# Attention output made transposed by column tiles of TensorE, the token scale moved to the last copy, no identity product, a new program order

## Chip, cores, metric

One core of one Trainium2 chip. The metric is device time in microseconds (us) of one execution; lower is better. Engines: PE is TensorE's matmul stream, PEld its weight loads, DVE the vector engine, ACT the scalar engine, POOL the general-purpose engine, SPq the queue that issues most DMA transfers.

## The reference, cut to what matters

```python
# attention: q, k, v, alpha of (4, 8, 768, 48); state is 48 x 48 for each batch and head
for t in range(S):
    state = alpha[:, :, t, :, None] * state + np.einsum('bhd,bhe->bhde', k[:, :, t], v[:, :, t])
    y[:, :, t] = np.einsum('bhd,bhde->bhe', q[:, :, t], state)
# x = y as 3072 tokens by 384 features
h = np.maximum(np.maximum(x @ w1, x @ w2), x @ w3)     # 384 -> 768
return h @ w_out                                        # 768 -> 384
```

## The kernel before

The sequence is cut into six chunks of 128 tokens and the batch into two pairs, which gives twelve steps; each step has two halves (u = 0, 1), one batch element with eight heads each. A step goes through PE in pieces: decay sums (`lps`), turning q and k (`tps`), scores (`aps`), attention output (`yps`), turning it back (`xtp`), state update (`sps`), the three gate products (`gps`, 54 matmuls of 256 columns) and the output product (`ops`). Program order on each engine is written out by hand in strings, one letter for each piece.

```python
    def attend(s, u):
        ...
        yps = ps.tile([P, HP, 2, D], FP32, name="yps", tag="s", bufs=2)
        for p in range(HP):                                  # four pairs of heads
            if cb > 0:
                nc.tensor.matmul(yps[:, p], qkT[:, 0, p, :], st[:, p, :], start=True, stop=False)
            for i in range(2):
                nc.tensor.matmul(yps[:, p, i, :], lat[:, i, p, :],
                                 vt[:, u * H + 2 * p + i, :],
                                 start=(cb == 0), stop=(cb == 0 or i == 1))
        xb = work.tile([P, DM], FP16, name="xb", tag="xb")
        nc.scalar.mul(xb, yps.rearrange("p a b d -> p (a b d)"), ys_c)   # token scale: one number per partition
        y_of[s, u] = xb

    def turn_back(s, u):
        ...
        for f in range(NF):
            nc.tensor.transpose(xtp[:, u, f, :], xb[:, f * P:(f + 1) * P], ident)
        if u == 1:
            ...
            nc.scalar.copy(out=xT.rearrange("p f u t -> p u f t"), in_=xtp_of.pop(s))

    def update(s, u):
        ...
        if cb > 0:                                           # the identity product: adds the old state
            nc.tensor.matmul(sps.rearrange("p a b d -> p (a b d)"), ident,
                             st.rearrange("p a b -> p (a b)"), start=True, stop=False)
        for p in range(HP):
            nc.tensor.matmul(sps[:, p], qk[:, 1, u * HP + p].rearrange("p a b -> p (a b)"),
                             vt[:, u * H + 2 * p:u * H + 2 * p + 2, :], ...)
        nc.vector.tensor_mul(stn..., sps, gm...)
    # ... cut ...
    STEADY = """N0 T0 S0 T1 G0 G1 D0 S1 O1 A0 O0 G2 A1 G3 Y0 G4 D1 G5 Y1 G6 X0 X1 G7 M0 V0 G8"""
    # ... cut ...
    load(1)          # load(0) stands further up; each loads alpha, k, q, v of one step
    load(2)
    load_weights()   # nine gate weights, three output weights
    load(3)
    load(4)
```

Of the kernel before, what the change touches and what calls it, by code (L numbers as in the profile page):

```python
# [9 lines left out]
FP32 = mybir.dt.float32  # L10
# [9 lines left out]
SIGMA = float(np.log(256.0))  # L20
# [3 lines left out]
def kernel(  # L24
# [17 lines left out]
    P = 128  # L42
    NCB = S // P
# [7 lines left out]
    assert DM == H * D and NT == B * S and 2 * D <= P  # L51
# [9 lines left out]
    c16_np = np.concatenate([tri_np, ident_np, mask_np, w2_np], 1)  # L61
    at = LAM * (rr - MID)
    c32_np = np.stack(
        [at, -at, np.exp(at + SIGMA), np.exp(-at - SIGMA), rr < 64, rr >= 64], 1
# [3 lines left out]
    raw = ctx.enter_context(tc.tile_pool(name="raw", bufs=4))  # L68
# [5 lines left out]
    ins = {n: t.rearrange("b h s d -> s b h d")  # L74
           for n, t in (("a", alpha), ("q", q), ("k", k), ("v", v))}
    raws = {}
# [4 lines left out]
    def load(s):  # L81
        cb, b0 = where(s)
        for n in ("a", "k", "q", "v"):
            t = raw.tile([P, NH, D], FP32, name=f"r{n}", tag=f"r{n}")
            nc.sync.dma_start(  # L85
                t, ins[n][cb * P:(cb + 1) * P, b0:b0 + U].rearrange("s b h d -> s (b h) d"))
            raws[s, n] = t

    c16 = cpool.tile([P, 3 * P + 2], FP16, name="c16")
    c32 = cpool.tile([P, 6], FP32, name="c32")  # L90
    load(0)
    nc.scalar.dma_start(c16, nc.inline_tensor(c16_np, name="c16").ap())
    nc.scalar.dma_start(c32, nc.inline_tensor(c32_np, name="c32").ap())
    tri, ident, mask, w2 = c16[:, :P], c16[:, P:2 * P], c16[:, 2 * P:3 * P], c16[:, 3 * P:]
    at_c, nat_c, vs_c, ys_c = (c32[:, i:i + 1] for i in range(4))
    half_c = c32[:, 4:6]


    NQ = 4
    las = [cpool.tile([P, NP, 2, 64], FP16, name=f"la{i}") for i in range(NQ)]  # L100
    qks = [cpool.tile([P, 2, NP, 2, 64], FP16, name=f"qk{i}") for i in range(NQ)]

    def clear_padding(i):
        nc.vector.memset(las[i].rearrange("p a b c -> p (a b) c")[:, :, D:], 0.0)
        nc.vector.memset(qks[i].rearrange("p i a b c -> p (i a b) c")[:, :, D:], 0.0)
# [3 lines left out]


    wcat = cpool.tile([P, NF, 3, DF], FP16, name="wcat")
    wo16 = cpool.tile([P, NJ, DM], FP16, name="wo16")
    wstage = []

    def load_weights():
        for jg in range(NJ // 2):
            for g, w in enumerate((moe_w1, moe_w2, moe_w3)):
                cs = slice(jg * 2 * P, (jg + 1) * 2 * P)
                t = cpool.tile([P, NF, 2 * P], FP32, name=f"ws{jg}_{g}")
                nc.sync.dma_start(t, w.rearrange("(f p) j -> p f j", p=P)[:, :, cs])  # L120
                wstage.append((wcat[:, :, g, cs], t))
        for i in range(3):
            js = slice(2 * i, 2 * i + 2)
            t = cpool.tile([P, 2, DM], FP32, name=f"wos{i}")
            nc.sync.dma_start(t, moe_w_out.rearrange("(j p) m -> p j m", p=P)[:, js])
            wstage.append((wo16[:, js], t))

    def cast_weights(_, i):
        for dst, src in wstage[3 * i:3 * i + 3]:
            nc.gpsimd.tensor_copy(out=dst, in_=src)  # L130

    qk_of, v_of, gate_of, qkT_of, lat_of, y_of, xtp_of, xT_of, hT_of, h_of = (
        {} for _ in range(10))

    def logs(s, _):
        la = las[s % NQ].rearrange("p a b c -> p (a b) c")
        nc.scalar.activation(out=la[:, :, :D], in_=raws.pop((s, "a")), func=AFT.Ln)

    def decays(s, u):

        la, qk = las[s % NQ], qks[s % NQ]
        laf = la.rearrange("p a b c -> p (a b) c")
        qk_of[s] = qk
        hs = slice(u * H, (u + 1) * H)
        lps = ps.tile([P, 512], FP32, name="lps", tag="w", bufs=2)
        nc.tensor.matmul(lps[:, :H * D], tri, laf[:, hs, :D], start=True, stop=True)  # L146
        if u == 1:
            for p in range(NP):
                nc.tensor.matmul(lps[:, H * D + 2 * p:H * D + 2 * p + 2],  # L149
                                 la[:, p].rearrange("p a b -> p (a b)"), w2,  # L150
                                 start=True, stop=True)
        ac = work.tile([P, H, D], FP32, name="ac", tag="ac")
        ic = work.tile([P, H, D], FP32, name="ic", tag="ic")
        lv = lps[:, :H * D].rearrange("p (h d) -> p h d", d=D)
        nc.scalar.activation(out=ic, in_=lv, func=AFT.Exp, bias=nat_c, scale=-1.0)  # L155
        nc.scalar.activation(out=ac, in_=lv, func=AFT.Exp, bias=at_c)  # L156
        qv, kv = (qk[:, i].rearrange("p a b c -> p (a b) c")[:, hs, :D] for i in range(2))
        eng = nc.vector if s < 3 else nc.gpsimd
        eng.tensor_mul(kv, raws[s, "k"][:, hs], ic)  # L159
        eng.tensor_mul(qv, raws[s, "q"][:, hs], ac)  # L160
        if u == 1:
            ge = work.tile([P, NP, 2], FP32, name="ge", tag="ge", bufs=6)
            nc.scalar.activation(
                out=ge, in_=lps[:, H * D:H * D + 2 * NP].rearrange("p (a b) -> p a b", b=2),
                func=AFT.Exp)
            gate_of[s] = ge

    def values(s, _):
        vt = work.tile([P, NH, D], FP16, name="vt", tag="vt", bufs=4)
        nc.scalar.mul(vt, raws.pop((s, "v")), vs_c)  # L170
        v_of[s] = vt

    def turn(s, u):

        qk = qk_of[s]
        tps = ps.tile([P, 2, HP, P], FP16, name="tps", tag="w", bufs=2)
        for i in range(2):
            for p in range(HP):
                nc.tensor.transpose(  # L179
                    tps[:, i, p, :],  # L180
                    qk[:, i, u * HP + p].rearrange("p a b -> p (a b)"), ident)
        qkT = work.tile([P, 2, HP, P], FP16, name="qkT", tag="qkT", bufs=3)
        nc.vector.tensor_copy(out=qkT, in_=tps)  # L183
        qkT_of[s, u] = qkT

    def scores(s, u):
        qkT = qkT_of[s, u]
        lat = work.tile([P, 2, HP, P], FP16, name="lat", tag="lat")
        aps = [ps.tile([P, HP, P], FP32, name=f"aps{i}", tag="w", bufs=2) for i in range(2)]
        for p in range(HP):  # L190
            for i in range(2):
                rows = slice(64 * i, 64 * i + D)
                nc.tensor.matmul(aps[i][:, p, :], qkT[rows, 1, p, :], qkT[rows, 0, p, :],  # L193
                                 start=True, stop=True)
        for i in range(2):
            nc.vector.tensor_mul(lat[:, i], aps[i],  # L196
                                 mask.unsqueeze(1).broadcast_to([P, HP, P]))
        lat_of[s, u] = lat

    def attend(s, u):  # L200
        cb, b0 = where(s)
        st, vt = sts[b0 + u][cb % 2], v_of[s]
        qkT, lat = qkT_of.pop((s, u)), lat_of.pop((s, u))
        yps = ps.tile([P, HP, 2, D], FP32, name="yps", tag="s", bufs=2)
        for p in range(HP):
            if cb > 0:
                nc.tensor.matmul(yps[:, p], qkT[:, 0, p, :], st[:, p, :],  # L207
                                 start=True, stop=False)
            for i in range(2):
                nc.tensor.matmul(yps[:, p, i, :], lat[:, i, p, :],  # L210
                                 vt[:, u * H + 2 * p + i, :],
                                 start=(cb == 0), stop=(cb == 0 or i == 1))
        xb = work.tile([P, DM], FP16, name="xb", tag="xb")
        nc.scalar.mul(xb, yps.rearrange("p a b d -> p (a b d)"), ys_c)  # L214
        y_of[s, u] = xb

    def turn_back(s, u):
        if u == 0:
            xtp_of[s] = ps.tile([P, U, NF, P], FP16, name="xtp", tag="s", bufs=2)
        xtp, xb = xtp_of[s], y_of.pop((s, u))  # L220
        for f in range(NF):
            nc.tensor.transpose(xtp[:, u, f, :], xb[:, f * P:(f + 1) * P], ident)  # L222
        if u == 1:
            xT = work.tile([P, NF, U, P], FP16, name="xT", tag="xT", bufs=3)
            nc.scalar.copy(out=xT.rearrange("p f u t -> p u f t"), in_=xtp_of.pop(s))  # L225
            xT_of[s] = xT

    gm_of = {}

    def gates(s, _):  # L230

# [7 lines left out]
    def update(s, u):  # L239

        cb, b0 = where(s)
        qk, vt = qk_of[s], v_of[s]
        gm = gm_of[s]
        st, stn = sts[b0 + u][cb % 2], sts[b0 + u][(cb + 1) % 2]
# [138 lines left out]
```

## Time and profile before

| | before |
|---|---|
| median, range of three runs | 170.75 us (170.47 to 171.71) |
| profiled span | 168.8 us |
| PE busy | 156.9 us, 93% |
| steady step | 11.93 us |
| first gate matmul | 30.51 us |

The page of the profile before. The digits are busy tenths in 40 slices of the span; PEclk is the granted TensorE clock in tenths.

```profile
PE 156.9 (93%) x1758; PEld 121.1 (72%) x1758; DVE 112.2 (66%) x185; ACT 99.0 (59%) x181; POOL 49.0 (29%) x72
...
PE   7955859999999999999999999999999999999992
...
PEclk9995675599999999999999999999999999999999
```

PE is full from the seventh slice to the last but one. Before that there are holes, and the granted clock is lower.

The table of busy time by stretch, before. Columns: stretch, its length, busy time of each engine with its count of instructions, granted clock, DMA share, GB/s.

```profile
core 0: us, PE busy (x) PEld busy (x) DVE busy (x) ACT busy (x) POOL busy (x), PEclk, DMA share, GB/s
...
10.00:20.00 10.00, 6.46 (x71) 4.23 (x72) 7.03 (x13) 4.80 (x9) 0.00 (x0) 0.67 1.38 218
20.00:30.60 10.60, 7.93 (x94) 5.60 (x92) 7.89 (x14) 7.17 (x13) 3.25 (x6) 0.66 1.01 274
...
87.40:99.35 11.95, 11.95 (x150) 9.64 (x148) 8.78 (x15) 8.13 (x16) 4.28 (x6) 1.00 1.03 207
```

In the steady stretch only PE is full, so there a microsecond saved on PE's stream is a microsecond saved, and a microsecond saved on another engine is worth nothing.

PE's timeline before, some of the groups that the change touches. Columns: start, duration from first start to last end, engine, line, operation, count. The durations overlap, because matmuls are pipelined: the cost of a group is the distance from its start to the start of the next.

```profile
89.64 0.82 PE L268 MATMUL gps_1589<-xT,wcat 128*128 128x256 f16 x6
90.39 0.23 PE L193 MATMUL aps_1598<-qkT 48*128 48x128 f16 x1
...
90.72 0.83 PE L268 MATMUL gps_1610<-xT,wcat 128*128 128x256 f16 x6
91.39 0.21 PE L207 MATMUL yps<-st_1_89,qkT 128*128 128x96 f16 x1
...
91.77 0.82 PE L268 MATMUL gps_1634<-xT,wcat 128*128 128x256 f16 x6
...
94.46 0.55 PE L222 MATMUL xtp<-c_68,xb 128*128 128x128 f16 x6
94.85 0.82 PE L268 MATMUL gps_1702<-xT,wcat 128*128 128x256 f16 x6
...
96.61 0.33 PE L247 MATMUL sps<-st_0_92,c_68 128*128 128x384 f16 x1
96.77 0.33 PE L250 MATMUL sps<-vt,qk_85 128*128 128x96 f16 x4
```

Six gate matmuls take 0.655 us (54 take 5.90). So the scores of one half cost 90.72 - (89.64 + 0.655) = 0.42 us, the gap before them included, and its attention output 91.77 - (90.72 + 0.655) = 0.395 us. Turning back costs 94.85 - 94.46 = 0.39 us per step, an identity product 96.77 - 96.61 = 0.16 us.

The queue's timeline before: the first weight is the thirteenth transfer.

```profile
21.73 1.52 SPq L120 DMA_DIRECT2D ws_0_114<-in_moe_w_dram  x1
```

### The profile page before, as it was taken

How to read it: one execution, taken by the hardware profiler on the slowest of the kernel's cores; microseconds unless marked ns; L12 is line 12 of the kernel's file. 1: busy time of each engine (PE TensorE's matmuls, PEld its weight loads, DVE VectorE, ACT ScalarE, POOL GpSimd, SP SyncE). 2: the span in 40 equal slices, each digit the busy share in tenths (PEclk: the TensorE clock that was granted, in tenths of full speed). 3: DMA queues.
4: the chain of work that ended last, by engine and by line, in shares of the span. 5: the costliest groups of instructions: out<-in, count | busy, mean ns of one | idle time of the engine just before them, and what ended most of it. 6: DMA issues, size and time to landing. Idle time of an engine off the chain costs nothing.

```text
span 168.8 us, 4329 instructions
## 1 busy us (share of the span) xinstructions
PE 156.9 (93%) x1758; PEld 121.1 (72%) x1758; DVE 112.2 (66%) x185; ACT 99.0 (59%) x181; POOL 49.0 (29%) x72
## 2 busy tenths in 40 slices
PE   7955859999999999999999999999999999999992
PEld 2423637699887676886877978968968869869860
DVE  4186777756647757597587587687667775975730
ACT  3616585142777684874974964956856748435232
POOL 0000005756063454404512531541442244100000
PEclk9995675599999999999999999999999999999999
DMA  6999999998999999999897967948931011020013
GB/s 131 223 219 218 176 247 336 355 360 170 226 172 213 218 248 254 192 226 221 219 223 189 235 105 177 228 91 192 212 92 50 0 56 41 0 93 4 0 47 140
DMA packets 107251, 28.68 MB, mean 170 GB/s; under 512 B 99808, under 2 KB 107232, under 8 KB 107232
## 3 DMA queue, kind: packets, MB, share of 16 engines
q1 hardware_dynamic: 106944, 28.32, 77.3%
q8 instruction: 13, 0.21, 0.6%
q10 hardware_dynamic: 288, 0.10, 0.3%
q14 instruction: 6, 0.05, 0.1%
HBM read 23.69 MB, written 4.72 MB: 168 GB/s over the span
## 4 chain that ended last, share of the span: by engine, by line
PE 81%; SPq 7%; DMA 3%; ACT 3%; DVE 2%; issue 1%; ACTq 0%
PE ops L285 14%; SPq L85 7%; PE tps L179 6%; DMA ra<-in_alpha_dram 3%; PE yps L210 3%; PE xtp L222 2%; PE lps L146 2%; PE yps L207 2%; PE sps L250 2%; PE sps L247 2%; DVE lat L196 1%; PE lps L149 1%; ACT xb L214 1%; PE gps_514 L268 1%; PE gps_523 L268 1%
## 5 line engine op out<-in xcount | busy, mean ns | idle before, releaser
L268 PEld LDWEIGHTS <-wcat 128*128 128x128 f16 x648 | 60.3, 98 | 9.0 <-POOL gm L235 0.2
L285 PE MATMUL ops<-wo_97,hT 128*128 128x384 f16 x144 | 27.1, 327 | 0.0
L288 ACT COPY ob<-ops 128x384 f32<-128x384 f32 x24 | 11.5, 480 | 14.2 <-PE ops L285 14.2
L155 ACT ACTIVATE ic<-lps,c_69 128x384 f32<-128x384 f32 x24 | 13.9, 581 | 8.4 <-PE lps L146 5.1
L285 PEld LDWEIGHTS <-hT 128*128 128x128 f16 x144 | 12.8, 98 | 7.5
L183 DVE COPY qkT<-tps 128x1024 f16<-128x1024 f16 x24 | 16.4, 683 | 1.3 <-PE tps L179 1.1
L214 ACT ACTIVATE xb<-yps,c_69 128x384 f16<-128x384 f32 x24 | 14.0, 585 | 4.8 <-PE yps L210 4.8
L156 ACT ACTIVATE ac<-lps,c_69 128x384 f32<-128x384 f32 x24 | 13.8, 575 | 0.0
L210 PE MATMUL yps<-vt,lat 128*128 128x48 f16 x192 | 12.2, 190 | 0.6 <-ACT vt L170 0.6
L193 PEld LDWEIGHTS <-qkT 48*128 48x128 f16 x192 | 6.3, 98 | 8.8 <-issue 7.7
L159 POOL TENSOR_TENSOR qk_87<-rk,ic 128x384 f16<-128x384 f32 x6 | 6.0, 997 | 21.9 <-ACT ic L155 21.9
L210 PEld LDWEIGHTS <-lat 128*128 128x128 f16 x192 | 10.5, 101 | 1.5 <-DVE lat L196 0.7
L170 ACT ACTIVATE vt<-rv,c_69 128x768 f16<-128x768 f32 x12 | 11.3, 940 | 0.0
L225 ACT COPY xT<-xtp 128x768 f16<-128x768 f16 x12 | 9.6, 803 | 1.0 <-PE xtp L222 1.0
L296 PE MATMUL wps<-blank 128*128 128x512 f16 x22 | 8.0, 528 | 1.2 <-DVE blank L343 1.2
L159 POOL TENSOR_TENSOR qk_86<-rk,ic 128x384 f16<-128x384 f32 x4 | 4.0, 997 | 15.4 <-ACT ic L155 15.4
L130 POOL CAST wcat<-ws_0_114 128x768 f16<-128x768 f32 x1 | 0.8, 823 | 26.3 <-DMA ws_0_114<-in_moe_w_dram 26.3
L159 POOL TENSOR_TENSOR qk_85<-rk,ic 128x384 f16<-128x384 f32 x4 | 4.0, 995 | 13.9 <-ACT ic L155 13.9
L207 PEld LDWEIGHTS <-qkT 128*128 128x128 f16 x80 | 7.7, 98 | 0.4
L222 PE MATMUL xtp<-c_68,xb 128*128 128x128 f16 x72 | 7.4, 228 | 0.5 <-ACT xb L214 0.3
L159 POOL TENSOR_TENSOR qk_84<-rk,ic 128x384 f16<-128x384 f32 x4 | 4.0, 996 | 12.4 <-ACT ic L155 12.4
L222 PEld LDWEIGHTS <-xb 128*128 128x128 f16 x72 | 5.2, 101 | 2.3 <-ACT xb L214 0.9
(409 smaller groups left out, 359.6 us busy)
## 6 DMA issues: line engine op xcount, KB each, us to landing
ra<-in_alpha_dram SPq DMA_DIRECT2D x12, 384.0 KB, 4.7
rk<-in_k_dram SPq DMA_DIRECT2D x12, 384.0 KB, 5.6
rq<-in_q_dram SPq DMA_DIRECT2D x12, 384.0 KB, 5.8
rv<-in_v_dram SPq DMA_DIRECT2D x12, 384.0 KB, 5.7
out_dram<-ob SPq DMA_DIRECT2D x24, 192.0 KB, 2.0
ws_0_114<-in_moe_w_dram SPq DMA_DIRECT2D x1, 384.0 KB, 4.9
ws_1_116<-in_moe_w_dram SPq DMA_DIRECT2D x1, 384.0 KB, 4.5
ws_2_118<-in_moe_w_dram SPq DMA_DIRECT2D x1, 384.0 KB, 5.0
```

The lines of the kernel that those rows point to most:

```text
L85: nc.sync.dma_start(t, ins[n][cb * P:(cb + 1) * P, b0:b0 + U].rearrange("s b h d -> s (b h) d"))
L155: nc.scalar.activation(out=ic, in_=lv, func=AFT.Exp, bias=nat_c, scale=-1.0)
L156: nc.scalar.activation(out=ac, in_=lv, func=AFT.Exp, bias=at_c)
L159: eng.tensor_mul(kv, raws[s, "k"][:, hs], ic)
L170: nc.scalar.mul(vt, raws.pop((s, "v")), vs_c)
L183: nc.vector.tensor_copy(out=qkT, in_=tps)
L210: nc.tensor.matmul(yps[:, p, i, :], lat[:, i, p, :], vt[:, u * H + 2 * p + i, :], start=(cb == 0), stop=(cb == 0 or i == 1))
L214: nc.scalar.mul(xb, yps.rearrange("p a b d -> p (a b d)"), ys_c)
L222: nc.tensor.transpose(xtp[:, u, f, :], xb[:, f * P:(f + 1) * P], ident)
L268: nc.tensor.matmul(gps[:, j, :], wcat[:, f, g, jj * P:(jj + 1) * P], xT[:, f].rearrange("p u t -> p (u t)"), start=(f == 0), stop=(f == NF ...
L285: nc.tensor.matmul(ops, hT_of[s][:, jj, u * P:(u + 1) * P], wo16[:, jj, :], start=(jj == 0), stop=(jj == NJ - 1))
L288: nc.scalar.copy(out=ob, in_=ops)
```

## The change

The intent: (1) make the attention output with features on the partitions at once, so that it need not be turned back. Features come in blocks of 32 (a pair of heads has 96), and each block is a product with 32 stationary columns that goes to one of four column tiles of PE. (2) With tokens now along the free axis, a scale per token is no longer one number per partition; it moves to the last copy, where tokens are on partitions again. The maxima in between are not affected by a positive factor. (3) The old state is added on DVE, not by an identity product. (4) Load order and program order are new: weights come in between the inputs, more warm-up matmuls stand in the prologue, and the two halves' scores, and the two halves' attention outputs, stand next to each other.

```diff
-SIGMA = float(np.log(256.0))
+SIGMA = float(np.log(16.0))
+    LOADS = """a1 a0 q0 w0 k0 k1 q1 w2 v0 a2 v1 w1
+        w3 w4 w6 w5 q2 k2 w7 w8 v2 a3 w11 w10
+        w9 q3 k3 v3"""
     # ... cut: the exponents' biases go into the scale of the logarithm ...
-        nc.scalar.mul(xb, yps.rearrange("p a b d -> p (a b d)"), ys_c)
-            nc.tensor.transpose(xtp[:, u, f, :], xb[:, f * P:(f + 1) * P], ident)
+        yps = bank([P, NF, P], "yps", tag or "s")
         for f in range(NF):
+            jobs = []
+            for c in range(P // C):
+                p, part = divmod(P // C * f + c, 3)
+                vp = vt[:, u * HP + p].rearrange("p a b -> p (a b)")
+                job = [] if cb == 0 else [(st[:, p, C * part:C * (part + 1)], qkT[:, 0, p, :])]
+                # ... cut: one or two products of v with lat ...
+                jobs.append(job)
+            for n in range(max(len(j) for j in jobs)):
+                for c, job in enumerate(jobs):
+                    if n < len(job):
+                        nc.tensor.matmul(yps[C * c:C * (c + 1), f, :], job[n][0], job[n][1],
+                                         start=(n == 0), stop=(n == len(job) - 1))
     # update
-            nc.tensor.matmul(sps.rearrange("p a b d -> p (a b d)"), ident,
-                             st.rearrange("p a b -> p (a b)"), start=True, stop=False)
+            nc.vector.tensor_add(full, sps_of.pop((s, u)), sts[b0 + u][cb % 2]...)
     # store
-        nc.scalar.copy(out=ob, in_=ops)
+        times(eng or "a", ob, ops_of.pop((s, u)), ys_c)
-    STEADY = """N0 T0 S0 T1 G0 G1 D0 S1 O1 A0 O0 G2 A1 G3 Y0 G4 D1 G5 Y1 G6 X0 X1 G7 M0 V0 G8"""
+    STEADY = """S1@-1 S0g@-1 N0@2 T1@1 t1@1 s0@-1 s1@-1 O0@-1 T0@1 G0@0 t0@1 G3@0
+        z0v@-1 A1@1 a2@1 A0g@1 z1p@-1 O1@-1 o0v@-1 h0@0 a0@1 c0@2 h3@0 G1@0
+        ... Y0@1 h1@0 h2@0 h4@0 f1@2 q0p@2 k0p@2 V0@2 Y1@1 G5@0 ..."""
     # ... cut: prologue, last step, pieces split into matmul and copy, v padded to 64 per head ...
```

In the strings a capital letter is a PE piece (G, O, T, A, Y, S) or an ACT one (N logarithm, V values); small letters are the copies that follow. `Y0` and `Y1` have only work of other engines between them, so on PE they are neighbours; likewise `A1` and `A0`.

## The prediction

> **What bounds the kernel now.** TensorE. The page has PE busy 93% of a 168.8 us span; the busy table by stretch shows PE busy 11.95 of 11.95 us in a steady step (87.4 to 99.35 us), against DVE 8.8, ACT 8.1, POOL 4.3. From start-to-start distances in PE's timeline a steady step is: 54 gate matmuls 5.90, output product 1.95, turning q and k 0.90, scores 2 x 0.42, attention output 2 x 0.395, decay sums 0.53, turning back 0.39, state update 2 x 0.33 (half of it the identity product): 11.96, the step found. So in the steady part only PE stream time counts. The rest is the start: gates begin at 30.6 us, because the first weight lands at 26.7 us behind twelve input loads, 1.75 us apart on the DMA queue; from 10 to 30 us the granted clock is 0.67. Of the 165.5 us to the last matmul about 141 are that stream, about 25 idle, warm-up or slow clock. The tail (3.3 us) stays.
>
> **What the change does.**
> - Removes turning back (0.39 us per step) and the identity product (2 x 0.163): -0.72. Both halves' scores now stand together: one pair of row-tile switches less, about -0.1 (a score group takes 0.42 us, its eight matmuls 0.25).
> - Attention output becomes 28 matmuls per half, 32 columns by 128, instead of 12. With four column tiles side by side, about nine rounds of 56 ns: 0.5 us per half. If the pairs of weight load and matmul follow one another at the 25 ns that the two-column sums show: 0.7. Both halves are back to back, so one switch in and out, about 0.2. Sum 1.2 to 1.7 against 0.79: +0.4 to +0.9. The Trainium skill, TensorEngine Tiling (Array Packing), Key Properties and Restrictions, says that changing the tiling mode drains the engine and that column tiling excludes Fast Weight Load; no trace here shows column tiles yet, the row-tiled scores agree with about 0.1 us per switch.
> - Steady step: 11.5 to 12.0 us, centre 11.7 (-2.5 us over ten steps).
> - The state sum goes to DVE (0.55 each), half the decays to POOL. DVE rises to 9.5 to 10.5 us of the step, ACT falls to about 7 (copies of 2 x 0.48 for 2 x 0.585 and 0.80). Neither should bound.
> - Loads: the first weights are 4th, 8th and 12th, landing near 10, 16 and 23 us by the same spacing (input 1.75, weight 1.13). Gates can start near 21 us and be dense from 24, with two steps' attention done before. Non-useful PE time falls from 25 to between 17 and 20: -5 to -8 us. 57 warm-up matmuls instead of 22 fill idle time and hold the clock.
>
> **Critical path.** The start and the steady PE difference lie on it wholly; the moved scale, copies and exponent biases do not.
>
> **Predicted time:** 162.0 us, 157.0 to 168.0 for 8 times in 10. Faster by over 2%: 0.87; within 2%: 0.10; slower: 0.03.
>
> **What would show each step.** First gate matmul at 20 to 22 us, dense by 25. Clock above 0.67 from 10 to 30 us. Steady step 11.5 to 12.0 us, PE still full, attention 1.2 to 1.7 us for both halves. Last matmul to end about 3.3 us.
>
> **What would make it wrong.** Column-tile weight loads that do not overlap (60 ns per pair would be 3.4 us per step: slower than before). DVE, near 10 of 11.7 us, becoming the one waited for, so that PE has gaps. Weights landing later than the spacing says, or the early order stalling on one late load. A better case: tiles fully side by side and no drain, a step near 11.2.

## The result, and the profile after

| | before | after |
|---|---|---|
| median (lowest to highest) of four runs each | 171.23 us (170.47 to 172.37) | 160.01 us (159.89 to 160.21) |
| profiled span | 168.8 us | 158.9 us |
| PE busy | 156.9 us, 93% | 150.5 us, 95% |
| steady step | 11.93 us | 11.27 us |
| first gate matmul | 30.51 us | 21.97 us |

The ratio is 0.9338, 95% interval 0.929 to 0.9387.

The page after:

```profile
PE 150.5 (95%) x2057; PEld 114.9 (72%) x2057; DVE 126.5 (80%) x210; ACT 78.5 (49%) x153; POOL 62.6 (39%) x87
...
PE   7999998979699999999999999999999999999991
...
PEclk9999999999999999999999999999999999999999
```

More matmuls and less PE time; DVE and POOL took work, ACT lost some. The early 9s of PE are mostly warm-up matmuls.

Busy time by stretch, after, with columns as above:

```profile
10.00:21.97 11.97, 11.39 (x148) 6.53 (x146) 9.00 (x14) 6.36 (x12) 6.00 (x6) 1.00 1.14 214
21.97:34.00 12.03, 10.60 (x136) 8.82 (x133) 9.00 (x16) 7.31 (x14) 5.90 (x8) 1.00 0.96 263
34.00:46.00 12.00, 10.43 (x159) 8.39 (x157) 8.50 (x14) 7.28 (x14) 4.24 (x6) 1.00 1.03 253
...
87.12:98.39 11.27, 11.27 (x174) 9.17 (x174) 10.49 (x18) 5.78 (x14) 5.09 (x8) 1.00 1.11 221
```

The steady step is still full on PE, with DVE at 10.49 of 11.27 us. Between 22 and 46 us PE lacks 1.4 and 1.6 us.

PE's timeline after, around one pair of scores and one of attention outputs:

```profile
91.90 1.47 PE L322 MATMUL gps<-xT,wcat 128*128 128x256 f16 x12
93.30 0.62 PE L235 MATMUL aps<-qkT 48*128 48x128 f16 x16
93.85 1.15 PE L346 MATMUL ops<-wo,hT 128*128 128x384 f16 x6
...
96.02 1.47 PE L322 MATMUL gps<-xT,wcat 128*128 128x256 f16 x12
97.42 0.24 PE L271 MATMUL yps<-qkT,st 128*32 128x128 f16 x4
97.49 0.23 PE L271 MATMUL yps<-lat,vt 128*32 128x128 f16 x4
...
97.83 0.23 PE L271 MATMUL yps<-qkT,st 128*32 128x128 f16 x4
...
98.32 1.92 PE L322 MATMUL gps<-xT,wcat 128*128 128x256 f16 x16
```

Twelve gate matmuls take 12 x 0.109 = 1.31 us. So the scores of both halves cost 93.85 - (91.90 + 1.31) = 0.64 us, where two separate groups cost 0.84; and attention of both halves costs 98.32 - (96.02 + 1.31) = 0.99 us, where it was 0.79 before plus 0.39 for turning back. The four tiles start together and each round takes about 0.06 us; the second half starts at 97.83, 0.41 us after the first, which is seven rounds.

The queue after; the first weight is the fourth transfer:

```profile
4.39 2.14 SPq L99 DMA_DIRECT2D ws<-in_moe_w_dram  x1
```

Where the ten microseconds went, from PE's timelines:

| part | before | after | difference |
|---|---|---|---|
| start, until the first piece of step 3 | 60.25 | 55.35 | -4.9 |
| eight steady steps, 3 to 10 | 95.24 | 90.13 | -5.1 |
| last step, until PE's last output product ends | 9.97 | 9.99 | 0.0 |

(Steps are counted from 0. Step 3 begins with its first turning or state product; the last step begins with its first gate matmul, at 155.49 us before and 145.48 us after; PE ends at 165.46 and 155.47 us.) The rest after PE's end is 3.3 and 3.4 us.

### The profile page after: what moved, and what is told of

The parts are those of the page before. It is cut to its first block, busy times and chain, and to the rows that moved or that the text cites. A ratio compares the mean times of both kernels' runs of the same rounds, so it can differ in the third digit from the quotient of the medians.

```text
span 158.9 us, 4886 instructions
## 1 busy us (share of the span) xinstructions
PE 150.5 (95%) x2057; PEld 114.9 (72%) x2057; DVE 126.5 (80%) x210; ACT 78.5 (49%) x153; POOL 62.6 (39%) x87
## 4 chain that ended last, share of the span: by engine, by line
PE 64%; SPq 20%; DMA 10%; ACT 3%; issue 1%
PE gps L322 36%; SPq L87 13%; PE ops L346 13%; DMA ra<-in_alpha_dram 10%; SPq L99 7%; PE yps L271 5%; PE tps L221 4%; PE aps L235 2%; PE sps L292 2%; PE lps L175 1%; ACT la L168 1%; PE lps L178 1%; ACT qkT L138 1%; ACT vt L144 1%; ACT xT L138 0%
## 5 line engine op out<-in xcount | busy, mean ns | idle before, releaser
L322 PE MATMUL gps<-xT,wcat 128*128 128x256 f16 x648 | 77.7, 273 | 0.7 <-POOL wcat L140 0.5
L248 DVE TENSOR_TENSOR lat<-aps,c 128x512 f16<-128x512 f32 x48 | 30.5, 681 | 1.1 <-PE aps L235 1.0
L138 ACT CAST h<-gps 128x512 f16<-128x512 f32 x25 | 14.5, 585 | 34.0 <-PE gps L322 33.5
L337 DVE TENSOR_TENSOR h<-gps,h 128x512 f16<-128x512 f32 x36 | 24.5, 684 | 7.0 <-ACT h L138 3.4
L203 POOL TENSOR_TENSOR qk<-rk,ic 128x384 f16<-128x384 f32 x19 | 19.7, 1036 | 25.7 <-ACT ge L196 20.8
L337 DVE TENSOR_TENSOR hT<-gps,h 128x512 f16<-128x512 f32 x36 | 24.7, 690 | 5.5 <-PE gps L322 3.4
L346 PE MATMUL ops<-wo,hT 128*128 128x384 f16 x144 | 26.9, 327 | 0.0
L203 POOL TENSOR_TENSOR qk<-rq,ac 128x384 f16<-128x384 f32 x21 | 21.7, 1037 | 11.2 <-ACT ge L196 7.0
L221 PE MATMUL tps<-c,qk 128*128 128x128 f16 x192 | 14.7, 219 | 1.2 <-DVE qk L203 0.9
L221 PEld LDWEIGHTS <-qk 128*128 128x128 f16 x192 | 11.9, 97 | 3.8 <-DVE qk L203 1.3
```

The source lines that it names most:

```text
L138: nc.scalar.copy(out=dst, in_=src)
L203: engines[eng or "p"].tensor_mul(dst.rearrange("p a b c -> p (a b) c")[:, :, :D], src[:, u * H:(u + 1) * H], dec)
L221: nc.tensor.transpose(tps[:, i, p, :], qk[:, u * NP + i * HP + p].rearrange("p a b -> p (a b)"), ident)
L248: nc.vector.tensor_mul(lat, aps_of[s, u][i], m)
L322: nc.tensor.matmul(gps[:, j, :], wcat[:, f, g, jj * P:(jj + 1) * P], xT[:, f].rearrange("p u t -> p (u t)"), start=(f == 0), stop=(f == NF ...
L337: nc.vector.tensor_max(h, gps, h_of[s, i - 1])
```

## The experiments

All are edits of the kernel after, but for one. Times are medians; ratios are against the kernel before on the same chip. The runs e1, e2, e3 and e8 on one chip and e4, e5, e6, e10 on a second had no unaltered kernel after beside them; after_again stood beside e7, e11 and e12 on a third. So a difference of some tenths of a us between times of different calls is not to be read; the steady steps can be compared.

| run | median us | ratio | interval | steady step us |
|---|---|---|---|---|
| e1_identity | 162.23 | 0.9542 | 0.9488 to 0.9596 | 11.59 |
| e2_old_attention | 162.78 | 0.9567 | 0.9516 to 0.9618 | 11.34 |
| e3_apart | 163.17 | 0.9598 | 0.9551 to 0.9645 | 11.70 |
| e8_tile_by_tile | 159.58 | 0.9386 | 0.9331 to 0.944 | 11.28 |
| e11_half_tokens (wrong result) | 157.21 | 0.9208 | 0.915 to 0.9266 | 10.95 |
| e7_no_scale (wrong result) | 160.14 | 0.9371 | 0.9305 to 0.9438 | 11.27 |
| e4_inputs_first | 168.25 | 0.9842 | 0.9791 to 0.9892 | 11.27 |
| e6_before_early_weights (edit of before) | 175.83 | 1.0273 | 1.0209 to 1.0337 | 11.93 |
| e5_no_warm | 159.07 | 0.9319 | 0.9265 to 0.9374 | 11.27 |
| e10_later_logs | 159.72 | 0.9347 | 0.9304 to 0.9389 | 11.27 |
| after_again (unaltered) | 160.37 | 0.9397 | 0.9332 to 0.9463 | 11.27 |
| e12_no_warm_later_logs | 159.36 | 0.9328 | 0.928 to 0.9376 | 11.27 |

### How far the start moves by itself

> The changed kernel unaltered, to have it on the same chip as the runs beside it, and to see how far its start moves from run to run. Expected 159.4 to 160.2 us, steady step 11.27; if the first steady output product (68.10 us in the first profile) moves by over 0.5 us, differences of that size in the start are not to be read from single profiles.

It came to 160.37 us (159.57 to 161.65), a little above the range expected, with the steady step as expected. The first piece of step 3 stands at 55.35 us in the first profile of this kernel, at 54.81 in this one, and at 54.22, 54.62 and 54.71 in three edits that leave the start as it was (e8, e7, e3). So differences of about 1 us in the start are not to be read from single profiles. This holds for the table above too: with these five profiles the start is 4.9 to 6.0 us shorter than in the one profile of the kernel before. The steady step, on the other hand, repeats to 0.01 us.

### The steady part: what each piece of the change is worth

> The changed kernel with the identity product put back into the state update (16 matmuls of 384 columns; the vector engine copies where it added, at the same size). Theory 1 (the steady step of 11.27 us is a full TensorE stream, so what is put into the stream is paid in full): a steady step grows by 2 x 0.163 = 0.33 us to 11.59 to 11.60, in all 16 x 0.163 = 2.6 us, so about 162.6 us. Rival (the step became shorter through the new order, through freed banks or through less work on the scalar engine, and TensorE has slack): the step stays at 11.27 and the time at 160.0.

```diff
+        if cb > 0:
+            nc.tensor.matmul(sps.rearrange("p a b d -> p (a b d)"), ident,
+                             sts[b0 + u][cb % 2].rearrange("p a b -> p (a b)"),
+                             start=True, stop=False)
...
-            nc.vector.tensor_add(full, sps_of.pop((s, u)), ...)
+        copy(eng or "v", full, sps_of.pop((s, u)))
```

The chain of waits of this run; the same output product, one step apart:

```profile
80.04 0.98 PE ops L347 x6
...
91.63 0.98 PE ops L347 x6
```

The step is 11.59 us, +0.32, and the time 162.23 us against 162.6 expected; e8, whose steady step is unchanged, took 159.58 on the same chip, 2.65 less. Theory 1 holds: what is put into PE's stream is paid in full. (The vector engine's work is the same, a copy for a sum, so this run prices the product and not the move to DVE, which is hidden as long as DVE stays under PE.)

> The changed kernel with the attention output made untransposed as before (12 matmuls of 128 columns per half), copied to fp16, turned back by six transposes and copied again; token scale left on the last copy. Theory 1 (stream sum): attention 0.79 and turning back 0.39 in place of 0.99 for both halves, +0.19 us per steady step, 11.46; over twelve steps 2.3 us, and up to 1.5 us more at the start where the new copies are waited for: 162.3 to 164. Rival (the transposed attention is the main gain of the steady part, nearly all of the 0.68 us by which a step became shorter): step about 11.9, 166 to 168 us.

```diff
+                nc.tensor.matmul(yps[:, p], qkT[:, 0, p, :], st[:, p, :], start=True, stop=False)
+            for i in range(2):
+                nc.tensor.matmul(yps[:, p, i, :], lat[:, i, p, :], vt[:, u * HP + p, i, :D], ...)
+    def keep_x ...: copy(eng or "a", xb_of[s, u], y_of.pop((s, u))...)
+    def turn_back ...: nc.tensor.transpose(xtp_of[s][:, u, f, :], xb[:, f * P:(f + 1) * P], ident)
+    def keep_xt ...: nc.scalar.copy(out=xT_of[s]..., in_=xtp_of.pop(s))
-    ... x1@1 G7@0 L0@4 h6v@0 h7@0 G8@0
+    ... x1@1 G7@0 X0@1 X1@1 L0@4 h6v@0 h7@0 y0@1 G8@0
```

PE's timeline of this run: old attention for both halves (first and last lines shown), then turning back.

```profile
86.99 0.21 PE L258 MATMUL yps<-st,qkT 128*128 128x96 f16 x1
...
87.69 0.21 PE L261 MATMUL yps<-vt,lat 128*128 128x48 f16 x2
87.74 2.12 PE L324 MATMUL gps<-xT,wcat 128*128 128x256 f16 x18
89.70 0.50 PE L276 MATMUL xtp<-c,xb 128*128 128x128 f16 x6
90.04 0.82 PE L324 MATMUL gps<-xT,wcat 128*128 128x256 f16 x6
```

The old form costs 0.75 + 0.34 = 1.09 us here, not 0.79 + 0.39: the same groups are cheaper where both halves stand together. So in the steady part the transposed form is worth only 0.07 us of a step (11.34 against 11.27; 11.46 was expected). The time is 162.78 us all the same, within what was expected, because of waits outside the steady part. Who waited for whom in this run (total us, times, longest):

```profile
PE xtp L276 <- ACT xb L138: 1.5, 2, 1.0
PE gps L324 <- ACT xT L280: 1.4, 3, 0.9
...
PE xtp L276 <- ACT full L138: 0.9, 1, 0.9
```

Its step 3 begins at 56.40 us, 1.0 to 2.2 us (on average 1.7) later than in the five profiles with the start unaltered. Of the 1.4 us that PE waits for the copy of the turned output, 0.9 fall at 42.5 us, before the first gate of the third step, and 0.2 before the last step's first gate, which starts 0.4 us after the gates ahead of it have streamed (147.28 less 146.23 + 0.655). So the transposed output's gain is that a matmul, a copy, a transpose and a copy became a matmul and a copy where the next product is already being waited for. One reservation: these new pieces were put into an order made for the other form; an order made for them might hide part of the 1.7 us at the start.

> The changed kernel with the two halves' score groups apart again (an output product between them) and the two halves' attention groups apart (a gate group between them), in the steady steps. Theory (each change of tile shape costs about 0.09 us on TensorE: the score pair became cheaper by 0.2 us per step only because it stands together): the steady step grows by 0.3 to 0.4 us (two more pairs of switches), 11.6, in all seven to eight steps 2.3 to 3 us: 162.3 to 163. Rival (the gap before a score group is a wait for its operands, not a switch): step within 0.05 of 11.27, time 160.0.

```diff
-        z0v@-1 A1@1 a2@1 A0g@1 z1p@-1 O1@-1
+        z0v@-1 A1@1 a2@1 O1@-1 A0g@1 z1p@-1
-        ... V0@2 Y1@1 G5@0 h5@0 x0@1 G6@0
+        ... V0@2 G5@0 Y1@1 h5@0 x0@1 G6@0
```

The step is 11.70 us, +0.43, and the time 163.17 us: slightly more than expected, and the rival falls. PE's timeline of this run shows both scores:

```profile
93.49 0.40 PE L235 MATMUL aps<-qkT 48*128 48x128 f16 x8
93.82 1.15 PE L346 MATMUL ops<-wo,hT 128*128 128x384 f16 x6
94.90 0.40 PE L235 MATMUL aps<-qkT 48*128 48x128 f16 x8
```

Each separate score group costs 0.42 us again (93.82 less 92.09 + 1.31), each separate attention group 0.59 (half of the pair's 0.99 would be 0.50). One switch from full tiles to row or column tiles and back costs about 0.2 us. The Trainium skill, TensorEngine Tiling (Array Packing), Key Properties, says that changing the tiling mode drains TensorE; this run agrees and gives the size. What fills the 0.2 us is not shown: at a switch the first weight load, 0.1 us long, isn't started ahead either (in the trace after, PEld stands idle for 0.21 us before the loads of a score or attention group).

Summed up, undoing one thing at a time: identity product 0.32, separate scores 0.20 to 0.21, old attention 0.07, together about 0.60 of the 0.66 us by which a step became shorter. The remaining 0.06 us is about what the order brings the old form too: old attention and turning back cost 0.79 + 0.39 = 1.18 us in the kernel before and 1.09 in e2.

### How the four column tiles run

> The changed kernel with the attention matmuls of one column tile issued one after another instead of round robin over the four tiles; the same 56 matmuls per step. Theory (four tiles run side by side only when consecutive matmuls in program order go to different tiles, and a matmul waits for the one before on its own tile): 33 rounds of 56 ns instead of 15 for both halves, +1.0 us per step, step 12.2 to 12.3 us, total 168 to 171. Rival (tiles overlap whatever the order, as each has its own queue, or each matmul costs a fixed issue time of about 16 ns): step 11.27, time 160.0.

```diff
-            for n in range(max(len(j) for j in jobs)):
-                for c, job in enumerate(jobs):
-                    if n < len(job):
+            for c, job in enumerate(jobs):
+                for n in range(len(job)):
```

The theory fell: step 11.28 us, time 159.58. In this kernel's program order the first tile's `st` product is followed by the first tile's `lat` product, and only then by the second tile's. The timeline, which is in order of start, has it otherwise:

```profile
84.55 0.25 PE L271 MATMUL yps<-qkT,st 128*32 128x128 f16 x4
84.61 0.24 PE L271 MATMUL yps<-lat,vt 128*32 128x128 f16 x4
84.67 0.22 PE L271 MATMUL yps<-qkT,st 128*32 128x128 f16 x1
```

The first products of all four tiles start before any second one. So matmuls of different column tiles did not start in program order; each tile worked through its own seven per half. The Trainium skill, TensorE: Matmul & The Clock Gate, Part 3, states that matmuls are "strict FIFO, no reordering" in start and end; for column tiles this run does not agree, and the time, which did not grow by the 1.0 us per step that strict order implies, says the same without relying on the trace's starts.

> Wrong result on purpose: every attention matmul of the changed kernel streams 64 tokens instead of 128, and the copy writes them twice. Theory (the four column tiles are bound by streaming: 14 matmuls per tile of 56 ns for both halves, 0.8 us, plus 0.18 for the switches): the attention of both halves falls from 0.99 to 0.55 to 0.65 us, the steady step from 11.27 to 10.85 to 10.95, time 156 to 157. Rival (each of the 56 weight load and matmul pairs costs a fixed 16 ns of issue, whatever it streams): attention stays at 0.99, step 11.27, time unchanged.

```diff
-                        nc.tensor.matmul(yps[C * c:C * (c + 1), f, :], job[n][0], job[n][1],
+                        nc.tensor.matmul(yps[C * c:C * (c + 1), f, :64], job[n][0], job[n][1][:, :64],
```

The result is wrong. In PE's timeline:

```profile
94.26 1.47 PE L323 MATMUL gps<-xT,wcat 128*128 128x256 f16 x12
95.66 0.21 PE L271 MATMUL yps<-qkT,st 128*32 128x64 f16 x4
...
96.23 2.03 PE L323 MATMUL gps<-xT,wcat 128*128 128x256 f16 x17
```

Attention of both halves falls to 96.23 - (94.26 + 1.31) = 0.66 us and the step to 10.95; the time, 157.21 us, is just above the range expected. So the tiles are bound by what they stream: 64 tokens fewer in 14 rounds save 0.33 us, where 14 x 64 columns at 0.109 / 256 us each are 0.38. The small rest stays open; a fixed cost per instruction is not what bounds the group.

### The moved token scale

> Wrong result on purpose: the last copy without the token scale. Theory (the scale on the last copy is off the critical path but for the very last one): copies 0.48 instead of 0.58 us on the scalar engine, time 0 to 0.2 us less than the changed kernel of the same call, the steady step unchanged at 11.27. Rival (the scale holds a PSUM bank longer and delays the next product): step shorter by 0.1 us, time 1 us less.

```diff
-        times(eng or "a", ob, ops_of.pop((s, u)), ys_c)
+        copy(eng or "a", ob, ops_of.pop((s, u)))
```

160.14 us against 160.37 of the unaltered kernel, with overlapping intervals, and the steady step 11.27 us. The copy itself fell from 0.58 us to 0.48 on ACT, as expected. In the steady step the scale is off the critical path; a difference in time is not shown.

### The start

> The changed kernel with its loads in the order: all inputs of the first three steps, then all weights, then the rest, as before the change (same transfers, same program order elsewhere). Theory (weights early in the load order are what lets gates start at 22 us): first gate matmul at 27 to 29 us, and as the gates of the first two steps then compete with nothing, the end moves by 3 to 5 us: 163 to 165. Rival (the start is limited by the total of bytes until step 3, or by the order of TensorE and the warm-up, not by which load comes first): 160 to 161.

```diff
-    LOADS = """a1 a0 q0 w0 k0 k1 q1 w2 v0 a2 v1 w1
-        w3 w4 w6 w5 q2 k2 w7 w8 v2 a3 w11 w10
+    LOADS = """a1 a0 q0 k0 k1 q1 v0 a2 v1 q2 k2 v2
+        w0 w2 w1 w3 w4 w6 w5 w7 w8 a3 w11 w10
         w9 q3 k3 v3"""
```

168.25 us: over eight microseconds lost, twice what was expected, and the first gate at 32.5 us. The waits say why the size was wrong, and ACT's timeline shows the holder:

```profile
PE yps L271 <- ACT vt L144: 10.1, 1, 10.1
```

```profile
26.90 0.83 ACT L138 CAST wcat<-ws 128x768 f16<-128x768 f32 x1 [12.38 <-DMA ws<-in_moe_w_dram]
27.63 0.93 ACT L144 ACTIVATE vt<-rv,c 128x768 f16<-128x768 f32 x1
```

The cast of the first weight stands on ACT ahead of the first values. These start right behind the cast, with no wait of their own; ACT works in program order, and so the late weight held everything behind it, for 12.4 us. In the stretch from 22 to 34 us PE was busy for 5.4 of 12 us, and its granted clock was 0.52. The run shows that this program order needs this load order; it doesn't measure the load order alone.

> The kernel before with the first three weight transfers moved ahead of the third step's inputs, all else as it was. Theory (early weights bring something only together with a program order that starts gates before the third step's attention; this kernel's TensorE waits for the third step's inputs before its first gate): the third step's inputs land about 3 us later, so 170.5 to 174 us. Rival (load order alone is the gain of the start): gates from about 26 us, 166 to 168 us.

```diff
     load(1)
+    load_weights(range(1), ())            # the first three
     load(2)
-    load_weights()
+    load_weights(range(1, NJ // 2), range(3))
```

175.83 us, 2.7% slower than before: worse than expected, and the rival (load order alone is the gain) falls. Again an in-order engine is the cause: the logarithm of the third step stands on ACT ahead of the second step's values, and its load now comes later. PE waits 4.9 us for those values, where it waited 0.6 before:

```profile
PE yps L210 <- ACT vt L170: 4.9, 1, 4.9
```

Taken together, the two runs show that with these two program orders early weights gain only where the order uses them. For the start, either half of this pair alone was a loss: step 3 begins at 63.68 us in e4 and at 65.09 in e6, against 60.25 before and 55.35 after. (As a whole e4 is still 1.6% faster than the kernel before: its steady step is the shorter one.)

> The changed kernel without its 57 warm-up matmuls. Theory (warm-ups keep the granted clock at full speed between 10 and 30 us, where it was 0.67 before): granted clock below 0.8 in the first 25 us, the early attention work and first gates at half speed, end 1 to 3 us later: 161 to 163. Rival (they only fill time in which TensorE waits for loads, so they cost and bring nothing): 159.5 to 160.3.

```diff
-    PROLOGUE = """N0@1 H5@0 H2@0 H2@0 H3@0 H5@0 H1@0 H6@0 N0@0 c1@0 c0g@0 f1@0
+    PROLOGUE = """N0@1 N0@0 c1@0 c0g@0 f1@0
     # ... and every other H piece of the prologue ...
```

159.07 us: my theory fell, and even the rival's range is undercut a little. In PE's timeline the early decay sums do take half as long again as in the unaltered kernel (0.48 us against 0.33), until about 22 us:

```profile
7.62 0.48 PE L175 MATMUL lps<-la,c 128*128 128x384 f16 x1 [7.62 <-ACT la L168]
...
21.41 0.45 PE L175 MATMUL lps<-la,c 128*128 128x384 f16 x1
...
22.55 0.33 PE L175 MATMUL lps<-la,c 128*128 128x384 f16 x1
```

So the clock was low, as the Trainium skill, TensorE: Matmul & The Clock Gate, Part 1, says it is until PE has been busy for a while. The profile's page gives a granted clock of 1.00 for this run all the same. That is a matter of reading: the packed trace has no clock record before 21.7 us, where one at full speed begins, and the page counts a stretch without a record as full speed. So the record agrees with the durations, and the page's 1.00 before 21.7 us says nothing. (With the warm-ups the record at full speed begins at 5.5 us.) And the slow clock cost nothing: before 22 us PE waits for loads, and the first gate matmul starts at 21.90 us, as with warm-ups.

> The changed kernel with the logarithm of the fourth step's decays, and of each step's later ones, placed later in the scalar engine's order, and the decay sums that need it after the first gates of the third step. Theory (the log waits for its load to 40.85 us and 59.84 us, and holds the copies behind it on the same engine, so that TensorE sits idle 1.3 us at 41 us and about 0.6 us in step 3; these gaps are scalar-engine order, not bytes): 1.5 to 2.4 us less, 157.6 to 158.6. Rival (the start is bound by bytes: any gap closed returns at the next load, the output weights or the fifth step's inputs): 159.5 to 160.2.

```diff
-        ... h7@1 N0@3 Y1@2 G8@1 c1@3 x0@2 h7@0 h8@0 c0@3 h8@1 x1@2 f0@3 f1@3 G0@2 G1@2 ...
+        ... h7@1 Y1@2 G8@1 x0@2 h7@0 h8@0 h8@1 x1@2 N0@3 G0@2 G1@2 c1@3 c0@3 f0@3 f1@3 ...
-    STEADY = """S1@-1 S0g@-1 N0@2 T1@1 ... h0@0 a0@1 ...
+    STEADY = """S1@-1 S0g@-1 T1@1 ... h0@0 N0@2 a0@1 ...
```

159.72 us, where 157.6 to 158.6 was expected. PE's wait for the logarithm fell from 1.5 us in the first profile to 0.2, but the time did not follow: the theory's size is refuted. That the gaps came back at the next loads is likely (the chain of waits goes through a later transfer of q), but only argued.

> The changed kernel with later logs and without the 57 warm-up matmuls, the two edits that each seemed to save 0.3 to 0.9 us. Theory (the start is bound by the landing of loads, so warm-ups bring nothing and gaps closed by the order are partly kept): 158.3 to 159.2 us, 0.5 to 1.0 us under the changed kernel of the same call. Rival (both savings were the chip, not the edit, and the start is bound by bytes): within 0.3 us of the changed kernel of the same call.

159.36 us (158.65 to 159.65) against 160.37 (159.57 to 161.65). The direction is as expected, but the intervals of the ratios overlap (0.928 to 0.9376, and 0.9332 to 0.9463), the median lies just above the range expected, and the start moves by itself by as much. It is at least no slower; that it is faster isn't shown.

## Why the prediction was right, and where it was not

The total was right: 162.0 us predicted, 160.01 measured, inside 157.0 to 168.0, and in the likeliest class. Two terms of the sum were mis-sized, in opposite directions; that they partly cancel, so that the total is only 2 us off, is luck.

- "Steady step: 11.5 to 12.0 us, centre 11.7 (-2.5 us over ten steps)". Measured 11.27, -5.1 us over eight steps. The mechanism (a full stream, so subtract and add) was right; e1 confirms it to 0.01 us per step. The mis-sized term is the attention group, "1.2 to 1.7" us for both halves, measured 0.99. Even its lower end, 2 x 0.5 + 0.2, was too high, because it counted "about nine rounds" per half (presumably three for each of the three blocks of 128 features, the most that any tile has in a block). The trace has seven (0.41 us per half): each tile runs through its own seven products without waiting for the others, as e8 confirms. The upper end allowed for weight loads and matmuls following one another at 25 ns, and for Fast Weight Load being excluded; of this nothing showed. A 32-column load shows 97 ns on the trace against 98 ns for a full one, and four tiles overlapped completely. Of the case named as better, "tiles fully side by side and no drain, a step near 11.2", the first half and the size came; the switches still cost their 0.2 us. A second small miss: scores standing together saved 0.20, not 0.1.
- "Non-useful PE time falls from 25 to between 17 and 20: -5 to -8 us". The whole start became 4.9 us shorter, and that includes the shorter stream of the first three steps (at most 3 x 0.66 = 2.0 us, an estimate from the steady step). The first gate came where predicted (20 to 22, measured 21.97). "Dense from 24" was the step that failed: PE lacks 3.0 us between 22 and 46 us, where it waits for the logarithm, the scaled q and k, and a weight cast, each behind its own load (1.3, 1.1 and 0.5 us).
- "57 warm-up matmuls instead of 22 fill idle time and hold the clock": they hold it, but in e5 nothing is lost without them.
- The identity product (0.33 predicted, 0.32 in e1), the tail (3.3 predicted, 3.4 measured), DVE (9.5 to 10.5 predicted, 10.5 measured) and the moved scale (e7) were as predicted. ACT fell further than predicted, to 5.8 us of a step, not "about 7".

The short description of the change puts the column tiles first. The experiments do not: of the 0.66 us saved in a steady step they bring 0.07, the missing identity product 0.32, the neighbouring scores 0.20. Their larger part lies at the start, where a copy and a transpose no longer stand between attention and gates: by e2 about 1.7 us there, with the reservation made above, against 8 x 0.07 = 0.6 us in the steady steps and about 0.4 before the last step's gates. How the rest of the start's gain divides between load order and program order is open.

## What to carry to other kernels

Where an engine's stream is full, price each edit by the distance between starts in the trace, and price a group in the order in which it will stand: two groups of an unusual tile shape cost 0.2 us less next to each other than apart. Load order and the program order of in-order engines are one design: moving transfers alone cost 2.7% in one kernel and 8 us in the other, each time because one instruction on ACT stood waiting ahead of work that was ready. Before adding warm-up work, ask whether the engine that it warms is the one waited for.

## What the Trainium skill lacked or had wrong

- TensorE: Matmul & The Clock Gate, Part 3: it says matmuls start strictly in program order. With column tiles they did not: issued tile by tile, the step stayed at 11.28 us (33 rounds in order would have added 1.0 us), and four tiles' first products started before any second one.
- TensorEngine Tiling (Array Packing), Key Properties: it names the drain at a change of tiling mode without a figure. Here one switch away from full tiles and back cost about 0.2 us (two more pairs: +0.43 us per step).
- TensorEngine Tiling (Array Packing), Restrictions: column tiling excludes Fast Weight Load, which led me to price in slower loads. The page gives no cost, and here none showed: 56 pairs of 32-column load and 128-column matmul took 0.99 us with the switches, and halving the streamed columns took it to 0.66.
- No page: how to read a profile's clock column before its first clock record. In e5 it reads 1.00 there, while one matmul shape took 0.48 us; it took 0.33 after the first record, at 21.7 us.
